# Pooling in block chains on GpSimd, two pooling steps moved, and eight weight pieces brought forward in a fused attention and MoE kernel

## The chip, the core and the metric

The kernel runs on one core of a Trainium2 chip. The metric is device time in microseconds (us) of one execution. The engines are named as the profile names them: PE (TensorE, matmul), PEld (its weight loads), DVE (VectorE), ACT (ScalarE), POOL (GpSimd) and SP (SyncE, which issues most DMAs). Each works through its own instructions in order; they wait for one another by semaphores.

## The reference

Three layers run one after the other. Attention pools keys and values by 8, the second layer sends each of 4608 tokens to one of 8 experts, the third is dense. Here is the reference with setup and argument handling cut.

```python
# attention: q, k, v are (8, 8, 576, 64), keys and values are averaged over 8 positions
k_p = k.reshape(B, H, Sp, pool, D).mean(axis=3)      # Sp = 72
v_p = v.reshape(B, H, Sp, pool, D).mean(axis=3)
scores = scale * np.matmul(q, k_p.transpose(0, 1, 3, 2))
attn = softmax(scores)
x = np.matmul(attn, v_p)                              # -> 4608 tokens x 512
# experts: each token goes to its best expert
logits = x @ w_gate
e_idx = np.argmax(logits, axis=1)
gate_w = softmax(logits)[token, e_idx]
eom = 1.0 / (1.0 + np.exp(-(x @ w_output_gate)))
for e in range(8):
    h = np.maximum(x[mask] @ w1[e], 0.0)              # 512 -> 1024
    out[mask] = gate_w * eom * (h @ w2[e])            # 1024 -> 512
# dense: w_in and w_out are float64 in memory
r = np.maximum(x @ w_in, 0.0)                         # 512 -> 2048
y = (s * (r * r) + b) @ w_out                         # 2048 -> 512
```

## The kernel before, in words

The order of the instructions on every engine is written by hand (a manual schedule); the framework only adds the semaphore waits.

**Attention** (function `attention`) loops over t = 0 to 39 in steps of one tile of 128 tokens. Four and a half tiles make a batch element b. A step of the loop transposes queries (`s1`), multiplies them with pooled keys and subtracts the row maximum (`s2`), takes the exponential, transposes it (`s3`), multiplies it with the masked values (`s4`) and divides (`s5`). Steps that prepare a batch element are put at a t by the list `sched`: `pool_k(b)` and `pool_v(b)` add the 8 positions of keys and values, in three halvings (512 to 256, to 128, to 64 columns) over five blocks of up to 128 partitions; `prep_k`, `prep_l` and `prep_v` transpose the result on PE; `mask_v` and `mask_g` write the masked values and gate columns that `s4` reads. Keys and values lie in two buffers each, `krs[b % 2]` and `vrs[b % 2]`, and a buffer's next load on the SP queue waits until it is pooled. For b = 0 and 1 the pooling is on DVE, three instructions over all blocks; for later b on POOL, where the helper `add` cuts each halving into instructions of at most 256 columns: five for the first halving, three for the second, then three (keys) or two (values). Three tiles after each group of tiles is through, a router (class `Router`) ranks the tokens by expert on DVE, a few instructions between the others; its first batch starts with lines 556 and 557.

**Experts** (function `experts`) runs 39 slots of 128 tokens with the data given (36 fixed, the rest under a condition). In a slot PE does the first product of slot i (24 matmuls of 512 columns), the second product of slot i-1 (24) and twelve transposes. POOL gathers the tokens of a later slot, loads the next expert's weights when the expert changes (line 838) and scatters the token order (`tok.order`, line 1161). Each of these DMAs is issued by POOL in its own order. Beside this, `db.step` (class `Doubles`) turns the dense layer's float64 weights into float32, piece by piece: per step one load by SP, one ACT, three DVE and two POOL instructions on 128x256 values (lines 937 to 954), and for a piece of `w_out` also a split into two parts on ACT and DVE (lines 813 and 814). `db.pieces` lists 12 pieces of `w_out` (`EARLY`), then 32 of `w_in`, then 20 of `w_out`. The first 44 are done in the expert slots: `side` calls `db.step` once in each slot and once more where i % 3 is 0. From slot 34 on `ahead` loads the dense layer's first tokens by transposing DMAs (line 1200), and after slot 35, before slot 36, it calls `dn.join` four times: two copies that put the halves of the words together (line 1210, one on ACT and one on DVE) and two multiplications (line 1213, DVE).

**Dense** (class `Dense`) runs 9 groups of 512 tokens, 16 steps f each. A step does 12 matmuls of the first product (`c1`), ReLU on ACT, square, scale and split on DVE and ACT, and 12 matmuls of the second product (`c2`) two steps later. In group 0 the steps f = 1 to `REST` each hold two more calls of `db.step`, one of them ahead of the last DVE instruction of `c1`; `REST` is half of the pieces that are left, plus one: 11. Steps 0 to 4 also reload and split the second half of `w_in` (`reload`). At f = `REST` the next group's tokens are loaded, and in the four steps after that they are joined on ACT and DVE and cut in two for PE. Later groups are joined on POOL.

Of the kernel before, what the change touches and what calls it, by code (L numbers as in the profile page):

```python
# [16 lines left out]
ALU = mybir.AluOpType  # L17
# [5 lines left out]
B, H, S, D = 8, 8, 576, 64  # L23
# [11 lines left out]
NBLK = 5  # L35
# [10 lines left out]
KB = 7 * SP // 4  # L46


def attention(ctx, tc, c, q, k, v, wg, wog, xd, lg, ro, spare, hooks):
    nc = tc.nc  # L50
# [7 lines left out]
    krs = [  # L58
        one.tile([KB, NBLK, POOL * D], F32, name="kr"),
        spare[0:KB, 0:NBLK * POOL * D].rearrange("p (j f) -> p j f", j=NBLK),  # L60
    ]
    vrs = [one.tile([P, NBLK, POOL * D], F32, name=f"vr{i}") for i in range(2)]
# [16 lines left out]
    def load_kv(b, src, dst, n, j0=0, j1=NBLK):  # L79
        rows = src[b].rearrange("h (s r) d -> (h s) (r d)", r=POOL)  # L80
        j2 = min(j1, 4)
        nc.sync.dma_start(
            out=dst[0:n, j0:j2, :], in_=rows[j0 * n:j2 * n].rearrange("(j p) f -> p j f", p=n)
        )
        if j1 == NBLK:
            nc.sync.dma_start(out=dst[0:H * SP - 4 * n, 4, :], in_=rows[4 * n:H * SP])
# [36 lines left out]
    kp = {}  # L123
    vp = {}
    vt = {}

    def add(eng, out, x, y, w):

        n = out.shape[1]
        step = n if eng is nc.vector else max(1, 256 // w)  # L130
        for j in range(0, n, step):
            o, a, b = [t[:, j:min(j + step, n)] for t in (out, x, y)]
            eng.tensor_tensor(out=o, in0=a, in1=b, op=ALU.add)

    def halve(eng, t):
        add(eng, t[:, :, 0:256], t[:, :, 0:256], t[:, :, 256:512], 256)
        add(eng, t[:, :, 0:128], t[:, :, 0:128], t[:, :, 128:256], 128)

    def pool_k(b, j0=0, j1=NBLK):
        eng = nc.vector if b <= 1 else nc.gpsimd  # L140
        t = krs[b % 2][:, j0:j1]
        if j0 == 0:
            kp[b] = p2.tile([KB, NBLK, 2, D], F32, tag="kp", name="kp")
        halve(eng, t)
        x, y = [t[:, :, i:i + 64].unsqueeze(2).to_broadcast([KB, j1 - j0, 2, D]) for i in (0, 64)]
        add(eng, kp[b][:, j0:j1], x, y, 128)

    def pool_v(b):
        eng = nc.vector if b <= 1 else nc.gpsimd
        t = vrs[b % 2]  # L150
        vp[b] = vps[b % 2]
        halve(eng, t)
        add(eng, vp[b][:, 0:NBLK], t[:, :, 0:64], t[:, :, 64:128], 64)

    def prep_k(b, parts=((0, 4, 0, 7),)):

        pr = ps.tile([P, 512], F32, tag="prep", name="prk")
        kb = kbd[b % 3]
        prv = pr[:, 0:7 * SP].rearrange("p (h s) -> p h s", s=SP)

        def part(j0, j1, h0, h1):
            for j in range(j0, j1):
                nc.tensor.transpose(
                    out=pr[:, KB * j:KB * j + KB], in_=kp[b][:, j].rearrange("p t d -> p (t d)"),
                    identity=ident[0:KB, 0:KB],
                )
            copy = nc.vector.tensor_copy if j0 else nc.scalar.copy
            nc.scalar.copy(out=kb[0:64, h0:h1, 0, :], in_=prv[0:64, h0:h1])
            copy(out=kb[64:P, h0:h1, 1, :], in_=prv[64:P, h0:h1])

        return [lambda a=a: part(*a) for a in parts]
# [211 lines left out]
    def at(i, f, *a):  # L383
        sched.setdefault(i, []).append((f, a))
# [20 lines left out]
    prep_l(0)  # L405
    load_q(4)
    load_kv(1, v, vrs[1], P)
    at(1, pool_v, 0)
    at(4, pool_v, 1)
    at(2, prep_v, 0)  # L410
    at(2, mask_v, 0, 0, NBLK)
    at(3, pool_k, 1)
    at_end = {3: [lambda: prep_k(1)[0](), lambda: prep_l(1)]}
    at(5, prep_v, 1)
    at(5, mask_v, 1, 0, 3)
# [459 lines left out]
CW = 256  # L875
AHEAD = 2
NDX = 6
EARLY = 12
LO64 = 2.0 ** -15
HI64 = 2.0 ** 17 * (1.0 - 2.0 ** -24) * 0.9375  # L880

# [1 line left out]
class Doubles:  # L883
# [5 lines left out]
    def __init__(self, tc, ctx, w_in, w_out, wi):  # L889
# [3 lines left out]
        self.wi, self.wo, self.wf = wi, [], None  # L893
        self.more(ctx, EARLY * CW // DM)
        self.src = [w.bitcast(I32) for w in (w_out, w_in)]
        out = [(0, r, c) for r in range(FF // P) for c in range(DM // CW)]
        self.pieces = out[:EARLY] + [(1, r, c) for c in range(FF // CW) for r in range(DM // P)] + out[EARLY:]
        self.x, self.t, self.stores = {}, {}, []
        self.run(0, EARLY + len(self.pieces) // 2)

# [425 lines left out]
def kernel(  # L1326
# [15 lines left out]
    nc = tc.nc  # L1342
# [6 lines left out]
    kp = {}  # L1349
# [60 lines left out]
    dn = Dense(tc, wide, half, wt.a, wt.b, db, s_b, ys, out, tok)  # L1410

    def side(i, part):
        ahead(i, part)
        if part == 0:
            if i == 0:
                close_ranks(tc, c, wide(), kp)
            db.step()
        else:
            if i == 3:
                token_scale(tc, wide(), lg, kp, tok.scale)  # L1420
            if i % 3 == 0:
                db.step()
            if i > 3:
                tok.order(kp["pos"], 1 + (i % 4 == 0))

    def ahead(i, part):

        k = 2 * (i - NT + 3) + part - 2
        if k == -1:
            tok.load(kp["pos"])  # L1430
        elif 0 <= k < 4:
            dn.load(0, k)
        elif k == 4:
            for k in range(4):
                dn.join(0, k, [nc.scalar, nc.vector])

    with ExitStack() as x:
        db.wf = x.enter_context(tc.tile_pool(name="wf", bufs=1)).tile([P, DM // P, FE], F32, name="wf")
# [39 lines left out]
```

## Time and profile before

| what | value |
|---|---|
| time, median of 3 executions | 1535.36 us (1525.38 to 1536.66) |
| the profiled execution's own time | 1536.34 us |
| its span, first to last instruction | 1534.7 us |
| PE busy | 1464.4 us (95%) |
| DVE busy | 815.2 us (53%) |
| ACT busy | 522.3 us (34%) |
| POOL busy | 497.3 us (32%) |
| mean granted TensorE clock | 0.982 |

Attention fills the span up to about 213 us, the expert slots go from 216 to 727 us, the dense layer from 734 to the end. Busy time is what the profiler records for an engine's instructions; PE's ends are modelled, so that PE can show as busy where it issues few matmuls, and the number of its instructions in a stretch tells more. An idle time in square brackets stands ahead of its instruction and names what ended it. PEclk is the share of full TensorE speed that was granted: 1.00 is 2.4 GHz, and the lower level is half of it.

### The profile page before, as it was taken

The page shows a single profiled execution, that of the slowest core. Times are in us where ns is not written, and L with a number is a line of the kernel's source. Part 1 is how long each engine was busy: PE and PEld are TensorE (multiplying, and loading weights), DVE is VectorE, ACT ScalarE, POOL GpSimd, SP SyncE. Part 2 cuts the span into 40 slices and gives each one's busy share as a digit, 9 for nine tenths or more (in the row PEclk, how much of TensorE's full clock was granted, in tenths as well). Part 3 has the DMA queues.
Part 4 walks back from the last instruction along what each step waited for, and adds up shares of the span by engine and source line. Part 5 has one row for each costly group of instructions (what it writes and reads, how often), then busy time and mean ns, then how long its engine had stood idle before and what let it go on. Part 6 is the DMA issues. An engine that isn't in the chain of part 4 may idle for free.

```text
span 1534.7 us, 21105 instructions
## 1 busy us (share of the span) xinstructions
PE 1464.4 (95%) x7264; PEld 1228.2 (80%) x7264; DVE 815.2 (53%) x1503; ACT 522.3 (34%) x984; POOL 497.3 (32%) x609
## 2 busy tenths in 40 slices
PE   5979999999799999997999999999999999999997
PEld 5879988877588888886877888888888888888886
DVE  5788884475544557333896434444444434444432
ACT  3546632353433344222543222222222222222221
POOL 3964233445554455400470304040220304040100
PEclk9999999999899999998999999999999999999998
DMA  9866352265544457372423101010010101000000
GB/s 253 286 196 201 118 199 84 70 227 179 152 124 116 136 145 239 86 70 61 144 66 86 28 14 42 21 42 21 28 35 15 35 14 42 15 28 1 28 1 28
DMA packets 127401, 141.02 MB, mean 92 GB/s; under 512 B 62174, under 2 KB 84958, under 8 KB 127262
## 3 DMA queue, kind: packets, MB, share of 16 engines
q1 hardware_dynamic: 111726, 89.28, 21.3%
q0 software_dynamic: 15536, 50.12, 10.3%
q8 instruction: 59, 0.97, 0.3%
q14 instruction: 80, 0.66, 0.2%
HBM read 98.67 MB, written 31.25 MB: 85 GB/s over the span
## 4 chain that ended last, share of the span: by engine, by line
PE 45%; DVE 4%; ACT 1%; issue 1%; DMA 1%; another core or an unknown queue 0%; SPq 0%; POOLq 0%; ACTq 0%; DVEq 0%
PE po L1273 8%; PE po L1272 8%; PE po L1271 8%; PE ph L1241 8%; PE ph L1242 8%; PE ph L1240 8%; DVE gl L1260 1%; DVE r L1245 1%; DVE r L1246 1%; DVE wo L814 1%; DMA wb<-wi 0%; DVE wb L814 0%; ACT dx L937 0%; DVE dt L949 0%; DVE dy L1213 0%
## 5 line engine op out<-in xcount | busy, mean ns | idle before, releaser
L1245 DVE TENSOR_TENSOR r<-r 128x512 f32<-128x512 f32 x144 | 108.9, 756 | 301.6 <-ACT r L1244 301.4
L1283 POOL DMA_INDIRECT out<-yo,kp_pos x36 | 37.1, 1031 | 588.5 <-ACT yo L1282 521.2
L1273 PE MATMUL po<-wo,gl 128*128 128x512 f32 x560 | 218.7, 391 | 1.8 <-DVE gl L1260 1.7
L1271 PE MATMUL po<-wo,gh 128*128 128x512 f32 x560 | 217.9, 389 | 0.0
L1272 PE MATMUL po<-wo,gh 128*128 128x512 f32 x560 | 217.9, 389 | 0.0
L1046 PE MATMUL py<-wb,hh 128*128 128x512 f32 x624 | 199.0, 401 | 14.1 <-ACT wb L813 7.8
L1244 ACT ACTIVATE r<-ph 128x512 f32<-128x512 f32 x144 | 85.7, 595 | 324.6 <-PE ph L1242 324.6
L1257 ACT ACTIVATE gh<-r 128x512 fp32r<-128x512 f32 x140 | 88.5, 632 | 216.7 <-DVE r L1246 216.7
L1046 PEld LDWEIGHTS py<-wb,hh 128*128 128x128 f32 x624 | 120.9, 194 | 43.4 <-ACT wb L813 9.1
L1260 DVE TENSOR_TENSOR gl<-r,gh 128x512 fp32r<-128x512 f32 x140 | 106.9, 764 | 90.5 <-ACT gh L1257 90.5
L1015 PE MATMUL ph<-wa,xh 128*128 128x512 f32 x312 | 126.7, 406 | 0.0
L1273 PEld LDWEIGHTS po<-wo,gl 128*128 128x128 f32 x560 | 105.1, 188 | 26.5 <-DVE gl L1260 4.8
L1016 PE MATMUL ph<-wa,xh 128*128 128x512 f32 x312 | 123.1, 395 | 1.6 <-DVE wa L814 1.6
L1017 PE MATMUL ph<-wa,xl 128*128 128x512 f32 x312 | 122.9, 394 | 0.0
L1046 PE MATMUL py<-wb,hl 128*128 128x512 f32 x312 | 122.7, 397 | 0.0
L1271 PEld LDWEIGHTS po<-wo,gh 128*128 128x128 f32 x560 | 105.2, 188 | 21.6
L1272 PEld LDWEIGHTS po<-wo,gh 128*128 128x128 f32 x560 | 105.0, 188 | 21.9
L1240 PE MATMUL ph<-xdh,wa 128*128 128x512 f32 x288 | 112.2, 389 | 1.8 <-ACT xdh L813 1.8
L1241 PE MATMUL ph<-xdl,wa 128*128 128x512 f32 x288 | 112.1, 389 | 0.3 <-DVE xdl L814 0.3
L1240 PE MATMUL ph<-xdh,wb 128*128 128x512 f32 x288 | 112.0, 389 | 0.0
L1242 PE MATMUL ph<-xdh,wa 128*128 128x512 f32 x288 | 112.0, 389 | 0.0
L1241 PE MATMUL ph<-xdl,wb 128*128 128x512 f32 x288 | 112.0, 389 | 0.0
(237 smaller groups left out, 2724.1 us busy)
## 6 DMA issues: line engine op xcount, KB each, us to landing
wr<-in_moe_w POOLq DMA_DIRECT2D x56, 512.0 KB
ys<-y SPq DMA_DIRECT2D x38, 256.0 KB
xd<-x SPq DMA_DIRECT2D x36, 256.0 KB
q<-in_q SPq DMA_DIRECT2D x16, 512.0 KB
vr<-in_v SPq DMA_DIRECT2D x8, 1024.0 KB
wr<-in_moe_w SPq DMA_DIRECT2D x16, 512.0 KB
dx<-in_moe_w_out SPq DMA_DIRECT2D x32, 256.0 KB
dx<-in_moe_w_in SPq DMA_DIRECT2D x32, 256.0 KB
```

The costliest lines, as they stand in the source:

```text
L1015: nc.tensor.matmul(ph, lhsT=xh[:, k], rhs=wh[:, k, s], start=k == 0, stop=False)
L1016: nc.tensor.matmul(ph, lhsT=xh[:, k], rhs=wl[:, k, s], start=False, stop=False)
L1017: nc.tensor.matmul(ph, lhsT=xl[:, k], rhs=wh[:, k, s], start=False, stop=k == 3)
L1046: nc.tensor.matmul(py, lhsT=a, rhs=w, start=j == 0, stop=j == len(steps) - 1)
L1240: nc.tensor.matmul(ph, lhsT=wh[:, k, s], rhs=xh[:, k], start=k == 0, stop=False)
L1241: nc.tensor.matmul(ph, lhsT=wh[:, k, s], rhs=xl[:, k], start=False, stop=False)
L1242: nc.tensor.matmul(ph, lhsT=wl[:, k, s], rhs=xh[:, k], start=False, stop=k == 3)
L1245: nc.vector.tensor_tensor(out=r, in0=r, in1=r, op=ALU.mult)
L1260: nc.vector.tensor_tensor(out=gl, in0=r, in1=gh.bitcast(F32), op=ALU.subtract)
L1271: nc.tensor.matmul(o, lhsT=gh[:, s], rhs=wh, start=f == 0, stop=False)
L1272: nc.tensor.matmul(o, lhsT=gh[:, s], rhs=wl, start=False, stop=False)
L1273: nc.tensor.matmul(o, lhsT=gl[:, s], rhs=wh, start=False, stop=f == NC - 1)
```

## The change

The helpers `add` and `halve` give way to `pooled`. On DVE it issues the same three instructions; on POOL it takes one block after the other and does all three halvings of a block in a row, so that each instruction reads what the one before it has written. Fifteen instructions do a batch element's keys or values on POOL, where eleven or ten did before. `pool_v(0)` moves from DVE (t = 1) to POOL, ahead of the loop. `pool_k(1)` stays on DVE and moves from t = 3 to t = 2. `EARLY` goes from 12 to 20: eight pieces of `w_out` move from the dense layer's first group into the expert slots, `REST` becomes 7, and `side` calls `db.step` a second time in two of three slots. The first four joins go to POOL.

```diff
-    def add(eng, out, x, y, w):
+    def pooled(eng, out, t):
         n = out.shape[1]
-        step = n if eng is nc.vector else max(1, 256 // w)
-        for j in range(0, n, step):
-            o, a, b = [t[:, j:min(j + step, n)] for t in (out, x, y)]
-            eng.tensor_tensor(out=o, in0=a, in1=b, op=ALU.add)
-
-    def halve(eng, t):
-        add(eng, t[:, :, 0:256], t[:, :, 0:256], t[:, :, 256:512], 256)
-        add(eng, t[:, :, 0:128], t[:, :, 0:128], t[:, :, 128:256], 128)
+        for j in [slice(0, n)] if eng is nc.vector else [slice(j, j + 1) for j in range(n)]:
+            o, a = out[:, j], t[:, j]
+            eng.tensor_tensor(out=a[:, :, 0:256], in0=a[:, :, 0:256], in1=a[:, :, 256:512], op=ALU.add)
+            eng.tensor_tensor(out=a[:, :, 0:128], in0=a[:, :, 0:128], in1=a[:, :, 128:256], op=ALU.add)
+            x, y = a[:, :, 0:64], a[:, :, 64:128]
+            if len(o.shape) == 4:
+                x, y = [i.unsqueeze(2).to_broadcast(list(o.shape)) for i in (x, y)]
+            eng.tensor_tensor(out=o, in0=x, in1=y, op=ALU.add)
...
-        eng = nc.vector if b <= 1 else nc.gpsimd
-        t = vrs[b % 2]
         vp[b] = vps[b % 2]
-        halve(eng, t)
-        add(eng, vp[b][:, 0:NBLK], t[:, :, 0:64], t[:, :, 64:128], 64)
+        pooled(nc.vector if b == 1 else nc.gpsimd, vp[b][:, 0:NBLK], vrs[b % 2])
...
-    at(1, pool_v, 0)
+    pool_v(0)
     at(4, pool_v, 1)
     at(2, prep_v, 0)
     at(2, mask_v, 0, 0, NBLK)
-    at(3, pool_k, 1)
+    at(2, pool_k, 1)
...
-EARLY = 12
+EARLY = 20
...
-            if i % 3 == 0:
+            if i % 3 != 2:
                 db.step()
...
-                dn.join(0, k, [nc.scalar, nc.vector])
+                dn.join(0, k, [nc.gpsimd, nc.gpsimd])
```

On POOL, the pooling of the keys of b = 2 (`kr` is the key buffer, `kp` its result) stood like this; in brackets is what an instruction waits for, and Pool there is an earlier instruction of POOL itself:

```order
L133 TENSOR_TENSOR kr<-kr 126x256 [waits DMAHW1_49,DMAHW0_49,DVE_49]
L133 TENSOR_TENSOR kr<-kr 126x256 x2
L133 TENSOR_TENSOR kr<-kr 126x256 [waits DMAHW2_49,DVE_49]
L133 TENSOR_TENSOR kr<-kr 126x256 [waits DMAHW2_49]
L133 TENSOR_TENSOR kr<-kr 126x2x128 [waits Pool_49] x2
L133 TENSOR_TENSOR kr<-kr 126x128 [waits Pool_49]
L133 TENSOR_TENSOR kp<-kr 126x256 [waits PE_49,Pool_49]
L133 TENSOR_TENSOR kp<-kr 126x256 [waits Pool_49]
L133 TENSOR_TENSOR kp<-kr 126x128 [waits Pool_49]
```

Now it stands like this, after the five chains of `pool_v(0)`:

```order
L133 TENSOR_TENSOR kr<-kr 126x256 [waits DMAHW1_49,DMAHW0_49,DVE_49]
L134 TENSOR_TENSOR kr<-kr 126x128 [waits Pool_49]
L138 TENSOR_TENSOR kp<-kr 126x128 [waits PE_49,Pool_49]
L133 TENSOR_TENSOR kr<-kr 126x256
L134 TENSOR_TENSOR kr<-kr 126x128 [waits Pool_49]
L138 TENSOR_TENSOR kp<-kr 126x128 [waits Pool_49]
L133 TENSOR_TENSOR kr<-kr 126x256
L134 TENSOR_TENSOR kr<-kr 126x128 [waits Pool_49]
L138 TENSOR_TENSOR kp<-kr 126x128 [waits Pool_49]
```

Before, a wait for POOL itself was for an instruction two or three places earlier; now it is for the one just ahead, twice in each block.

On DVE, around the loop's steps t = 1 to 3 (`vr` and `vp` are the values, `wr` the keys of b = 1, `vbd` the masked values and gates, `mx` and `es` the maximum and the difference of one tile each), the order was:

```order
L133 TENSOR_TENSOR vp_154<-vr_140 128x320
L294 TENSOR_REDUCE mx<-sc 128x8
L297 TENSOR_TENSOR es<-sc,mx 128x576
L206 TENSOR_SCALAR vbd_147<-vp_154,msk 128x64 x4
L225 TENSOR_TENSOR vbd_147<-pf,msk 128x2x16
L225 TENSOR_TENSOR vbd_147<-pf,msk 128x3x16 x3
L225 TENSOR_TENSOR vbd_147<-pf,msk 128x16
L294 TENSOR_REDUCE mx<-sc 128x8
L297 TENSOR_TENSOR es<-sc,mx 128x576
L133 TENSOR_TENSOR wr_116<-wr_116 126x5x256
L133 TENSOR_TENSOR wr_116<-wr_116 126x5x128
L133 TENSOR_TENSOR kp<-wr_116 126x640
```

and is now:

```order
L288 TENSOR_REDUCE mx<-sc 128x8
L291 TENSOR_TENSOR es<-sc,mx 128x576
L200 TENSOR_SCALAR vbd_147<-vp_154,msk 128x64 x4
L133 TENSOR_TENSOR wr_116<-wr_116 126x5x256
L134 TENSOR_TENSOR wr_116<-wr_116 126x5x128
L138 TENSOR_TENSOR kp<-wr_116 126x640
L219 TENSOR_TENSOR vbd_147<-pf,msk 128x2x16
L219 TENSOR_TENSOR vbd_147<-pf,msk 128x3x16 x3
L219 TENSOR_TENSOR vbd_147<-pf,msk 128x16
L288 TENSOR_REDUCE mx<-sc 128x8
L291 TENSOR_TENSOR es<-sc,mx 128x576
```

The list before begins with the last of the three instructions of `pool_v(0)`; all three have left DVE. Those of `pool_k(1)` (`wr` and `kp`) came after the five instructions of `mask_g` (`vbd` from `pf`) and one more pair of `mx` and `es`; now they come ahead of them.

On ACT, between slots 35 and 36 of the experts (`xh` and `y` belong to slot 35's work, `hs` is the ReLU of slot 36's first product, the branch opens slot 36), the order was:

```order
L813 ACTIVATE xh_2787<-pt 128x512
L993 COPY y<-py 128x512
L1210 COPY dy<-dy 128x512 x4
L1125 COMPARE_AND_BRANCH
L1019 ACTIVATE hs_2790<-ph 128x512
```

and is now:

```order
L859 UNCONDITIONAL_BRANCH x2
L807 ACTIVATE xh_2853<-pt 128x512
L987 COPY y<-py 128x512
L1119 COMPARE_AND_BRANCH
L1013 ACTIVATE hs_2856<-ph 128x512
```

The four copies of the joins have left ACT; DVE loses its four copies and eight multiplications at the same place, and POOL has all sixteen ahead of its branch.

## Rows read from the trace of the kernel before

**Rows 1.** Busy time by stretch; instruction counts in brackets

```profile
core 0: us, PE busy (x) PEld busy (x) DVE busy (x) ACT busy (x) POOL busy (x), PEclk, DMA share, GB/s
0.00:40.00 40.00, 23.04 (x121) 21.13 (x122) 24.03 (x52) 13.28 (x30) 15.08 (x44) 0.91 0.98 254
400.00:440.00 40.00, 33.77 (x148) 27.25 (x147) 17.03 (x27) 12.54 (x21) 15.74 (x18) 0.87 0.56 170
680.00:720.00 40.00, 34.34 (x153) 28.18 (x152) 13.39 (x25) 9.50 (x16) 1.97 (x3) 0.91 0.31 79
840.00:880.00 40.00, 40.00 (x178) 33.10 (x178) 16.72 (x23) 9.13 (x15) 15.22 (x18) 1.00 0.13 37
```

**Rows 2.** Timeline of PE, attention: start, us, what, idle before and releaser

```profile
22.86 0.55 PE L193 MATMUL prv<-ident,vp 128*128 128x128 f32 x3 [2.56 <-DVE vp L133]
33.04 0.65 PE L163 MATMUL prk<-ident,kp 126*128 126x126 f32 x4 [2.32 <-DVE kp L133]
86.53 3.63 PE L344 MATMUL pv<-vbd,eT 128*128 128x162 f32 x12 [8.77 <-DVE vbd L225]
92.53 1.96 PE L344 MATMUL pv<-vbd,eT 128*128 128x162 f32 x12
123.11 0.49 PE L193 MATMUL prv<-ident,vp 128*128 128x128 f32 x3
```

**Rows 3.** Timeline of DVE, attention

```profile
19.94 2.34 DVE L133 TENSOR_TENSOR vr<-vr 128x1280 f32<-128x1280 f32 x2
29.78 2.34 DVE L133 TENSOR_TENSOR wr<-wr 126x1280 f32<-126x1280 f32 x2
32.16 0.83 DVE L133 TENSOR_TENSOR kp<-wr 126x640 f32<-126x640 f32 x1
75.32 9.54 DVE L557 TENSOR_TENSOR rcand<-lg,rmx 128x64 f32<-128x64 f32 x1
121.58 0.26 DVE L557 TENSOR_TENSOR rcand<-lg,rmx 128x64 f32<-128x64 f32 x1
```

**Rows 4.** Timeline of POOL, attention

```profile
33.25 5.23 POOL L133 TENSOR_TENSOR kr<-kr 126x256 f32<-126x256 f32 x8 [23.39 <-DMA kr<-in_k]
84.36 0.42 POOL L187 COPY kbm<-kbd 64x288 f32<-64x288 f32 x1
```

**Rows 5.** POOL groups by line and shape, first 560 us

```profile
L133 POOL TENSOR_TENSOR vr<-vr 128x256 f32<-128x256 f32 x42 | 29.0, 729 | 0.2
L133 POOL TENSOR_TENSOR vr<-vr 128x128 f32<-128x128 f32 x6 | 2.8, 460 | 0.0
L133 POOL TENSOR_TENSOR vp<-vr 128x64 f32<-128x64 f32 x6 | 1.9, 324 | 0.0
```

**Rows 6.** Timeline of POOL, one later join of the dense stage

```profile
846.24 1.45 POOL L1210 COPY dy<-dy 128x512 uint16<-128x512 uint16 x2
847.77 1.88 POOL L1213 TENSOR_TENSOR dy<-dy,ds 128x256 f32<-128x256 f32 x2
849.60 1.64 POOL L1210 COPY dy<-dy 128x512 uint16<-128x512 uint16 x2
```

**Rows 7.** Timelines of PE and ACT around the first joins

```profile
694.59 1.12 PE L1029 MATMUL th<-ident,hs 128*128 128x128 f32 x4 [4.81 <-ACTq L865]
696.56 1.12 PE L1029 MATMUL th<-ident,hs 128*128 128x128 f32 x4 [0.86 <-DVEq L865]
...
690.82 0.76 ACT L1210 COPY dy<-dy 128x512 uint16<-128x512 uint16 x1 [5.13 <-DMA dy<-ys]
693.95 0.58 ACT L1019 ACTIVATE hs<-ph 128x512 f32<-128x512 f32 x1
```

**Rows 8.** Busy time in the last part of the first dense group

```profile
785.00:826.00 41.00, 38.78 (x167) 30.52 (x166) 34.72 (x70) 18.34 (x38) 14.94 (x15) 1.00 0.37 80
```

**Rows 9.** Timelines of POOL and DVE, expert stage

```profile
405.43 0.99 POOL L1161 DMA_INDIRECT tab<-tok,kp_pos  x1 [4.97 <-DMA tab<-tok,kp_pos]
...
410.54 0.84 DVE L945 TENSOR_SCALAR dt<-dt 128x256 int32<-128x256 int32 x1 [5.10 <-POOL dt L939]
```

More of the change, by code (lines that the diff above doesn't have):

```diff
@@ L125, in attention @@
     vt = {}
-    def add(eng, out, x, y, w):
+    def pooled(eng, out, t):
         n = out.shape[1]
-        step = n if eng is nc.vector else max(1, 256 // w)
-        for j in range(0, n, step):
-            o, a, b = [t[:, j:min(j + step, n)] for t in (out, x, y)]
-            eng.tensor_tensor(out=o, in0=a, in1=b, op=ALU.add)
-    def halve(eng, t):
-        add(eng, t[:, :, 0:256], t[:, :, 0:256], t[:, :, 256:512], 256)
-        add(eng, t[:, :, 0:128], t[:, :, 0:128], t[:, :, 128:256], 128)
+        for j in [slice(0, n)] if eng is nc.vector else [slice(j, j + 1) for j in range(n)]:
[6 more added lines that the diff above has]
+            eng.tensor_tensor(out=o, in0=x, in1=y, op=ALU.add)
     def pool_k(b, j0=0, j1=NBLK):
-        eng = nc.vector if b <= 1 else nc.gpsimd
-        t = krs[b % 2][:, j0:j1]
         if j0 == 0:
             kp[b] = p2.tile([KB, NBLK, 2, D], F32, tag="kp", name="kp")
-        halve(eng, t)
-        x, y = [t[:, :, i:i + 64].unsqueeze(2).to_broadcast([KB, j1 - j0, 2, D]) for i in (0, 64)]
-        add(eng, kp[b][:, j0:j1], x, y, 128)
+        pooled(nc.vector if b <= 1 else nc.gpsimd, kp[b][:, j0:j1], krs[b % 2][:, j0:j1])
     def pool_v(b):
-        eng = nc.vector if b <= 1 else nc.gpsimd
-        t = vrs[b % 2]
         vp[b] = vps[b % 2]
-        halve(eng, t)
-        add(eng, vp[b][:, 0:NBLK], t[:, :, 0:64], t[:, :, 64:128], 64)
+        pooled(nc.vector if b == 1 else nc.gpsimd, vp[b][:, 0:NBLK], vrs[b % 2])
     def prep_k(b, parts=((0, 4, 0, 7),)):
```

## The prediction

> **What bounds the kernel now.** I first read the page's busy shares: PE 95%, no other engine above 53%. So the question is where PE is held up, and I went through the windows of 40 us, then the timelines of PE around each hole. In the dense layer a full stretch looks like 840 to 880 us: 178 matmuls in 40 us, 0.225 us each, clock 1.00 [rows 1]. Three kinds of stretch fall short. At the front PE is busy for 23.0 of 40 us; at 400 to 440 it issues few matmuls at a clock of 0.87; at 680 to 720 it is busy 34.3 us at 0.91 [rows 1]. The timeline of PE gives the holes of attention: 2.56 us for the pooled values of b = 0, 2.32 us for the pooled keys of b = 1, and 8.77 us for a gate column from DVE [rows 2]. After the last one the twelve matmuls of `s4` take 3.63 us, where the same twelve take 1.96 us a step later [rows 2]: the lower clock level for a while.
>
> The timeline of DVE explains them. The first two holes are DVE's own pooling: 2.34 us and a last halving for the values, 2.34 + 0.83 = 3.2 us for the keys [rows 3]. The third hole is one small comparison of the router, line 557 with 128x64 values: 9.54 us, where its next run takes 0.26 [rows 3]. It begins at 75.32 and ends at 84.86; POOL changes from two-input additions to a one-input copy at 84.36, and that copy ends at 84.78 [rows 4]. So I read the 9.5 us as DVE waiting for POOL's train of additions.
>
> **Part 1, chains.** By the means of one block on POOL, 0.73, 0.46 and 0.32 us [rows 5], and a wait for the instruction just ahead, a block of values takes longer than its three instructions. What such a wait costs shows in a later join: two copies from 846.24 take 1.45 us, and the multiplication that needs both starts at 847.77, 0.08 us after their end [rows 6]. A block is then 0.73 + 0.08 + 0.46 + 0.08 + 0.32, about 1.65 us, and b's values 8.2 us; keys end with 128 columns instead of 64 and take about 9. Before, the first two halvings were 5.2 us [rows 4] and the last one to two more. Each pooling on POOL grows by almost 2 us, and POOL is idle for at least 0.08 us after two of every three instructions.
>
> In those gaps a waiting DVE instruction can go ahead. Then the 8.77 us of PE go, and the slow matmuls behind it, 3.63 - 1.96 = 1.67 us: 10.4 us. The cost is that POOL gets late. Its chains can't start before 33.25, when the keys of b = 2 land [rows 4]. From there to the values of b = 5 there are eight poolings, 4 x 17.2 = 68.8 us, and eight copies of 0.42 [rows 4], with their waits some 4 us: 106 us. PE wants them at 123.11 now [rows 2]; with 10.4 us of this part and 4.5 of the next gone, at 108. The cover is 2 us, so each wait of DVE's additions against POOL shows soon. I charge 1.5 us. **-9.0**; bounds: 0 if the stall stays, -10.4 if POOL is never late.
>
> Here a rule of the Trainium skill speaks against the reading. "SBUF - State Buffer", section "Who interferes with whom", says that a DVE instruction with two SBUF inputs and a GpSimd instruction that reads SBUF share a port, and that the one that issues first holds it for its whole instruction. By this DVE would wait for one addition, at most 0.73 us, and not 9.54 across a dozen; then something else held line 557 and this part would bring nothing. The row differs from the rule in length, not in kind, and the end of the stall at the end of the train makes me go by the row; the rest is rival A.
>
> **Part 2, first values on POOL, second keys sooner.** About 1.7 MB of keys and queries and 1.2 MB of values come first; at 254 GB/s [rows 1] they are in at about 12 us (estimate). POOL is free from 33.25 - 23.39 = 9.9 us [rows 4], so the chain ends near 20.5 instead of 22.8, and the first hole shrinks by some 2.3 us. DVE then has `pool_k(1)`, 3.2 us, ahead of `mask_g` for `s4(0)`; PE loses about 0.9 us there. The second hole, 2.32, goes, since the keys are pooled by about 26. That makes -3.7, and the front's clock of 0.91 [rows 1] will give some of it back, say 0.8. **-4.5**; bounds: if the values landed as late as DVE takes them now (19.94 [rows 3]), the chain would end at 28 and the first hole grow by 5, so +1 in all; at best -7.
>
> **Part 3, first joins on POOL.** ACT's copy at 690.82 had waited 5.13 us for a transposing load; behind it in ACT's order stood slot 36's ReLU, which ran at 693.95, and PE's transposes of it waited 4.81 us, and 0.86 us more for the half that DVE makes [rows 7]. That is 5.67 us, and the clock of 0.91 over 40 us [rows 1] means about 7 us at half speed, 3 us of work or a little more: 8.5 us. On POOL the same join takes 849.60 - 846.24 = 3.4 us [rows 6], four of them 13.4 us. If the loads land no later than now, POOL is done by about 707. The cut of the joined tiles comes after slot 38, two slots later, so I count about ten us of cover. Behind the joins on POOL stands the gather of a slot that isn't used before the end. PE has no other wait for POOL there. **-8.5**; bounds 0 and -9.
>
> **Part 4, eight pieces less in the dense layer's first group.** DVE sets the pace there: 785 to 826 has 167 matmuls in 41 us [rows 8], where a full stretch would have 182 [rows 1], 15 short, 3.4 us. With `REST` = 7 the double steps of `db` end before this stretch, the joins of group 1 come four steps sooner, and PE's own matmuls bound it. What the first steps lose with `reload` stays. **-3.5**; bounds -1 and -6.
>
> **Part 5, the same pieces in the expert slots.** In slots of the usual kind PE hides them: DVE works about 17 of 40 us even at 400 to 440 [rows 1]. But in that stretch experts change almost each slot and POOL is late already: a scatter waited 4.97 us for an older one, and DVE's step at 410.54 waited 5.10 us for POOL's half of an earlier step [rows 9]. Two or three more steps fall here, each with two POOL instructions in front of scatters and weight loads. I take **+3**, between nothing (the weights' transfers bound these slots anyway) and +10 (each extra step holds a weight load for one such wait of 5 us, twice).
>
> The sum is -9.0 - 4.5 - 8.5 - 3.5 + 3 = -22.5 us. From the profiled execution's 1536.3 us this gives **1514 us**. That execution stands 1 us above the median of the three; one of the three was 10 us faster, and I can't tell which of the holes it lacked.
>
> **The rivals.**
> A. The stall of the comparison stays, because POOL's train was not its cause or because DVE loses the port all the same. For it: other DVE instructions get through POOL's trains quickly. Against it: the end at 84.36 to 84.86. Part 1 is then +1.5 instead of -9: about 1524 us. The skill's rule above leads here.
> B. The expert slots lose as much as their bound, +10 instead of +3, and a little more from slots with a lone change of expert: about 1522 us. For it: POOL late at 405 us. Against it: most of those waits are for transfers, which don't grow.
> C. A wait for the instruction just ahead costs POOL far more than 0.08 us, and POOL becomes what attention waits for. There are 80 of them up to the values of b = 5. With e us more for each, POOL is 80e late, less 2 us of cover; from e = 0.3 on this eats the 22 us gain. If a wait cost as much as the second halving, 0.46 [rows 5], e is 0.38 and PE stands for 28 us: about 1542 us, slower than before. Against it: the 0.08 of rows 6.
> D. The joins' loads land so late on POOL's side that the cut after slot 38 waits in the place of slot 36, and part 3 gives nothing: about 1522 us. Against it: the cover of two slots.
>
> **How the numbers follow.** Forecast 0.64 (its own range 1504 to 1520), A 0.13, B 0.11, C 0.05, D 0.07. The range of 1502 to 1527 takes in A, B and D as well as both bounds of parts 2, 4 and 5, and leaves out C and combinations of two rivals. A measurement of this kernel can tell about 1%, 15 us. The forecast lies 1.4% below 1535.4, and only its slow edge comes within 1%; A, B and D lie within 1% of the median. Faster by over 1%: 0.64. Within 1%: 0.30. Slower: 0.06, which is C and a little for several things at once.
>
> **What would show it.** Part 1: line 557's first run takes under 2 us, PE has no hole over 3 us between 60 and 100 us, and the POOL instructions of a chain start about 0.08 us after one another's end. Where POOL is late, PE's transposes of pooled keys or values name POOL as what ended their idle time. Part 2: PE's first hole under 1 us, the second gone. Part 3: no idle time at the transposes of slot 36, and POOL's joins done well before the cut. Part 4: PE at full count from about the tenth step of the dense layer on. Part 5: the sum of PE's idle time between 320 and 450 us, where more than 10 us over now would make rival B true. The forecast is wrong if attention is not at least 9 us shorter, or if the step from slot 36 to slot 37 still takes over 14 us.

## The result and the profile after

The changed kernel takes 1515.6 us, the median of 7 runs (1513.15 to 1519.97); the kernel before, run beside it, 1533.87 (7 runs, 1525.38 to 1537.30). The ratio is 0.9901 with a 95% interval of 0.9871 to 0.9930: 1% faster, 18.3 us by the medians. The profiled execution took 1513.15 us with a span of 1511.5, against 1536.34 and 1534.7. The forecast was 1514. The total is right; two of its five terms are off by about 4 us and two more by 2 to 3, and most of what follows is about these. The forecast took its 22.5 us off the profiled execution's 1536.3, while the median of the kernel before was 1533.87 here, so that 2.4 us of the agreement lie in the starting point.

Where the 23.2 us between the two profiled spans lie, by the first matmul of each stage in the timeline of PE (us from the span's start, the differences worked out):

| | before | after | difference |
|---|---|---|---|
| attention, to slot 0's first expert matmul | 216.40 | 206.94 | -9.46 |
| slots 0 and 1 | 21.11 | 20.26 | -0.85 |
| slots 2 to 35 | 441.10 | 440.68 | -0.42 |
| slots 36 and 37 | 33.06 | 24.49 | -8.57 |
| from slot 38 to the first dense matmul | 22.85 | 23.75 | +0.90 |
| dense, to the end | 800.22 | 795.36 | -4.86 |

The four stretches of [rows 1] in the changed kernel, and the one of [rows 8] at the same distance from the first dense matmul (busy time by stretch; the counts in brackets are instructions):

```profile
core 0: us, PE busy (x) PEld busy (x) DVE busy (x) ACT busy (x) POOL busy (x), PEclk, DMA share, GB/s
0.00:40.00 40.00, 23.69 (x141) 21.33 (x141) 24.92 (x55) 15.22 (x35) 21.62 (x56) 0.96 0.97 252
400.00:440.00 40.00, 34.39 (x157) 28.17 (x158) 21.20 (x36) 13.82 (x24) 23.59 (x24) 0.91 0.52 180
680.00:720.00 40.00, 37.09 (x166) 30.55 (x165) 17.18 (x23) 14.32 (x23) 8.63 (x11) 0.91 0.23 72
...
766.60:807.60 41.00, 41.00 (x183) 33.95 (x182) 22.29 (x40) 14.01 (x24) 0.00 (x0) 1.00 0.22 52
```

The front issues 141 matmuls where it issued 121. The dense stretch has 183 where it had 167, and PE shows no idle time in it.

The router's comparison (line 557 before, 551 now) took 9.54 us [rows 3]. In the timelines of DVE and POOL after, it and the router's next two-input instruction read:

```profile
73.55 0.26 DVE L551 TENSOR_TENSOR rcand<-lg,rmx 128x64 f32<-128x64 f32 x1
...
73.93 0.53 DVE L555 TENSOR_TENSOR rcand<-rcand,desc 128x64 f32<-128x64 f32 x1
...
73.66 0.72 POOL L133 TENSOR_TENSOR kr<-kr 126x256 f32<-126x256 f32 x1
74.46 0.46 POOL L134 TENSOR_TENSOR kr<-kr 126x128 f32<-126x128 f32 x1
```

The comparison takes its 0.26 us. Line 555, 0.21 us where nothing is in its way, takes 0.53 and ends at 74.46, at the end of POOL's idle time between 74.38 and 74.46. So a wait for POOL is still there, and it lasts to the next gap of the chain. The chain is as forecast: an instruction starts 0.08 us after the one it waits for has ended.

PE in attention, after. These answer [rows 2]:

```profile
21.02 0.33 PE L187 MATMUL prv<-ident,vp 128*128 128x128 f32 x1 [0.31 <-POOL vp L138]
...
26.07 2.05 PE L338 MATMUL pv<-vbd,eT 128*128 128x162 f32 x12 [1.39 <-DVE vbd L219]
...
61.60 2.02 PE L338 MATMUL pv<-vbd,eT 128*128 128x162 f32 x12 [1.60 <-DVE x L366]
...
98.55 0.46 PE L276 MATMUL sc<-kbm,qT 128*64 128x144 f32 x2 [1.01 <-POOL kbm L182]
99.51 1.19 PE L276 MATMUL sc<-kbm,qT 128*64 128x144 f32 x14 [0.50 <-POOL kbm L182]
```

The holes of 2.56, 2.32 and 8.77 us are gone. In the first's place stands 0.31 us, `mask_g` costs 1.39, and there are three new ones, at 60, 97 and 99 us. The second and third name a product of POOL that the prediction had counted only as time: the copies `kbm` of `prep_m`. The hole at 60 us leads to SP. DVE's line 366 waits for a store of `x` to leave its tile, and SP had spent 6.48 us on that store (timelines of DVE, SP and POOL):

```profile
60.76 0.69 DVE L366 TENSOR_TENSOR x<-pv,rec 128x512 f32<-128x512 f32 x1 [1.89 <-DMA xd<-x]
...
46.48 6.48 SPq L369 DMA_DIRECT2D xd<-x  x1
53.06 0.38 SPq L82 DMA_DIRECT2D vr<-in_v  x1
...
51.40 0.32 POOL L138 TENSOR_TENSOR vp<-vr 128x64 f32<-128x64 f32 x1
```

The load behind the store wants blocks that POOL is done with at 51.72, before the store's own time ends at 52.97. So it is not shown that POOL's lateness held the store; what did stays open. The expectation of `later` below reads this row as a wait for POOL.

The first joins, now on POOL, and PE's transposes of slot 36, which answer [rows 7]:

```profile
685.09 1.43 POOL L1207 TENSOR_TENSOR dy<-dy,ds 128x256 f32<-128x256 f32 x2
...
678.89 1.03 PE L1023 MATMUL th<-ident,hs 128*128 128x128 f32 x8
```

All eight transposes run in one go. POOL is done with the four joins at 686.5, two slots ahead of the cut.

### The profile page after: what moved, and what is told of

It is laid out like the page before. It is cut to its first block, busy times and chain, and to the rows that moved or that the text cites. A ratio compares the mean times of both kernels' runs of the same rounds, so it can differ in the third digit from the quotient of the medians.

```text
span 1511.5 us, 21197 instructions
## 1 busy us (share of the span) xinstructions
PE 1455.3 (96%) x7264; PEld 1224.2 (81%) x7264; DVE 794.6 (53%) x1488; ACT 520.4 (34%) x980; POOL 525.9 (35%) x694
## 4 chain that ended last, share of the span: by engine, by line
PE 50%; DVE 1%; ACT 0%; issue 0%; DMA 0%; POOLq 0%; ACTq 0%
PE po L1267 8%; PE ph L1236 8%; PE ph L1234 8%; PE ph L1235 8%; PE po L1265 8%; PE po L1266 8%; PE py L1040 1%; DVE r L1239 0%; DVE wb L808 0%; DVE gl L1254 0%; DVE wo L808 0%; DVE r L1240 0%; DMA out<-yo,kp_pos 0%; ACT dx L931 0%; ACT wo L807 0%
```

## Experiments

Each kernel below is the changed kernel with the edit shown, but for `chains`, which starts from the kernel before. Not all of them ran on the same chip, so the ratio to the runs of the kernel before on the same chip stands with each time.

| kernel | median us | runs | ratio to before, 95% interval | slot 0 begins | slots 2 to 35 | slots 36, 37 | dense |
|---|---|---|---|---|---|---|---|
| changed | 1515.60 | 7 | 0.9901 (0.9871 to 0.9930) | 206.94 | 440.68 | 24.49 | 795.36 |
| `train` | 1520.75 | 10 | 0.9949 (0.9920 to 0.9978) | 212.93 | 442.80 | 24.49 | 796.08 |
| `pairs` | 1523.72 | 10 | 0.9954 (0.9925 to 0.9983) | 218.00 | 441.11 | 24.49 | 795.40 |
| `breaks` | 1534.54 | 10 | 1.0022 (0.9995 to 1.0049) | 226.86 | 440.99 | 24.49 | 795.40 |
| `later` | 1513.54 | 7 | 0.9898 (0.9864 to 0.9932) | 201.72 | 441.37 | 24.49 | 795.40 |
| `joins` | 1523.43 | 10 | 0.9947 (0.9921 to 0.9974) | 208.49 | 438.71 | 32.60 | 795.82 |
| `firsts` | 1518.24 | 10 | 0.9899 (0.9874 to 0.9924) | 207.18 | 444.94 | 24.49 | 796.25 |
| `pieces` | 1513.92 | 4 | 0.9878 (0.9822 to 0.9935) | 208.39 | 434.96 | 24.49 | 800.91 |
| `chains` | 1521.05 | 10 | 0.9921 (0.9891 to 0.9952) | 206.80 | 435.42 | 32.78 | 800.32 |
| `again` | 1516.61 | 6 | 0.9908 (0.9872 to 0.9944) | 208.81 | 442.82 | 24.49 | 795.96 |
| `copies` | 1513.08 | 6 | 0.9895 (0.9857 to 0.9933) | 204.20 | 440.70 | 24.49 | 795.40 |
| `later_again` | 1514.59 | 6 | 0.9900 (0.9864 to 0.9936) | 202.48 | 441.68 | 24.49 | 795.63 |
| `spread` | 1517.12 | 8 | 0.9922 (0.9891 to 0.9952) | 203.79 | 447.70 | 24.49 | 796.43 |

The last four columns are from the one profiled execution of each, in us; "dense" is from its first matmul to the end. The expectations below count the slots one lower from the second on: their "slots 1 to 35" are the column of 2 to 35, their "35 to 37" that of 36 and 37.

### What holds the comparison: `train`, `pairs`, `breaks`

`train` has the old order by stages on POOL, one block to an instruction:

```diff
-        for j in [slice(0, n)] if eng is nc.vector else [slice(j, j + 1) for j in range(n)]:
-            (three halvings of block j)
+        for g in [[slice(0, n)]] if eng is nc.vector else [[slice(j, j + 1) for j in range(n)]]:
+            for s in range(3):
+                for j in g:
+                    (halving s of block j)
```

> The changed kernel, but POOL pools stage by stage over all five blocks again (five additions of 256 columns, five of 128, five last ones), so that an instruction never waits for the one just ahead of it; the rest of the change stays. Theory (an unbroken train of two-input additions on POOL holds a DVE instruction with two SBUF inputs until the train ends): of the router's first instructions on DVE, about 73 to 85 us, one takes over 5 us again, PE has a hole of more than 5 us there with a slow stretch behind it, and the time is 1515.6 + 7 to 10 = about 1523 to 1526 us. Rival A (the train was not the cause): none of them takes over 1 us, POOL is 1 to 2 us earlier at each pooling, and the time is 1512 to 1516.

The hold is back, on another instruction. In the timelines of DVE, POOL and PE of `train`:

```profile
82.21 7.21 DVE L627 CAST rri<-rrank 128x8 int32<-128x8 f32 x1
...
88.98 0.41 POOL L181 COPY kbm<-kbd 64x288 f32<-64x288 f32 x1
89.45 0.43 POOL L182 COPY kbm<-kbd 64x288 f32<-64x288 f32 x1
...
91.60 3.57 PE L338 MATMUL pv<-vbd,eT 128*128 128x162 f32 x12 [6.94 <-DVE vbd L219]
```

A cast of 8 columns, 0.16 us at other times, takes 7.21 and ends at 89.42. POOL's 14 additions and the copy behind them follow one another without idle time; the first is the 0.06 us between 89.39 and 89.45, where the second copy waits for the first. The hold ends in it. In the kernel before, the 9.54 us ended in such a gap too: POOL's first copy ends at 84.78 [rows 4], DVE's comparison at 84.86, and between them POOL's next copy starts:

```profile
84.84 0.42 POOL L188 COPY kbm<-kbd 64x288 f32<-64x288 f32 x1
```

In `train` PE has its hole of 6.94 us and then the twelve matmuls at the lower clock level, 3.57 us as in [rows 2]. Rival A falls. The price is 6.0 us of attention in the profile (4.1 against `again`) and 5.2 us by the medians, or 7.4 by the ratios; of the 7 to 10 expected that is the low end or less. Without links POOL is earlier, and PE has no hole at 97 us in `train`: undoing the chains also gives back what they cost.

`pairs` keeps nearly the order of the chains, but no instruction waits for the one just ahead:

```diff
+        for g in ... [[slice(j, j + 1) for j in g] for g in ((0, 1), (2, 3, 4))]:
+            for s in range(3):
+                for j in g:
+                    (halving s of block j)
```

> The changed kernel, but POOL's blocks are pooled in two interleaved groups (blocks 0 and 1, then 2, 3 and 4: each stage of a group before its next stage). An addition then waits for the one two or three ahead, which has ended, and POOL has no idle 0.08 us; the order is still nearly block by block. Theory that the idle gaps let DVE in: the gaps of 0.08 us are gone from POOL's rows, the hold is back at more than 4 us in one of DVE's instructions of the router, and the time is 1520 to 1526. Rival (the new order of the blocks, or the shift in time, did it, and not the gaps): no DVE instruction of the router over 1 us, each pooling about 1 us shorter than in chains, 1512 to 1516.

```profile
76.05 5.58 DVE L551 TENSOR_TENSOR rcand<-lg,rmx 128x64 f32<-128x64 f32 x1
...
78.16 3.31 POOL L138 TENSOR_TENSOR vr<-vr 128x256 f32<-128x256 f32 x6
```

The comparison is held for 5.58 us, another instruction of the router (line 562) for 3.72, and at 129.53 a step that splits expert weights (line 844) takes 2.52 instead of 0.68. POOL's six additions from 78.16 on take 3.31 us with no idle time between them. So it is not the order of the blocks or their place in time that helps: it is the 0.08 us in which POOL is idle. The two long holds end at 81.64 and 87.64, where POOL has no gap. PE also had a hole of 4.38 us at 58 us here, of the kind at 60 us above.

`breaks` takes the order of `train` and puts a copy of one column, which waits for no addition, behind each:

```diff
+                    if eng is nc.gpsimd:
+                        eng.tensor_copy(out=brk[:, 1:2], in_=brk[:, 0:1])
```

> The changed kernel with the stage by stage order of the run 'train', and behind each of POOL's additions a copy of one column (one input, 128x1), which does not wait for the addition. Theory 1 (a waiting DVE instruction gets in as soon as POOL runs something other than a two-input addition): no DVE instruction of the router over 1 us; a pooling costs 7 us plus 15 small copies of some 0.1 us, as long as in chains, and the time is 1513 to 1517. Theory 2 (only an idle POOL lets it in): one DVE instruction over 5 us, 1521 to 1527.

```profile
118.35 8.48 DVE L555 TENSOR_TENSOR rcand<-lg,rmx 128x64 f32<-128x64 f32 x1
...
125.86 0.73 POOL L138 TENSOR_TENSOR vr<-vr 128x256 f32<-128x256 f32 x1
126.52 0.19 POOL L140 COPY brk<-brk 128x1 f32<-128x1 f32 x1
126.66 0.49 POOL L138 TENSOR_TENSOR vr<-vr 128x128 f32<-128x128 f32 x1
```

Theory 2 holds: changing to a one-input instruction lets nothing in. DVE was held three times, the longest past 13 of the small copies: for 8.48 us, and two others took 3.97 and 3.23 us. The long hold ends at 126.83 with no idle time on POOL. It got in beside an addition that took 0.49 us instead of 0.45. So without a gap DVE does get in at some point, here and in `pairs` after 3 to 8.5 us; what decides when stays open. Each copy puts the next addition off by 0.12 us, almost 2 us to a pooling, and the kernel is as slow as the one before.

### Part 1 alone: `chains`

The kernel before with the new `pooled` and nothing else (values of b = 0 on DVE).

> The kernel before with the chains alone: part 1. Theory of the prediction: no hold of a DVE instruction over 1 us in attention, POOL late by little, slot 0's first expert matmul at 216.4 - 9 = 207.4 us, time 1533.9 - 9 = 1525. Rival (the chains make POOL late, and the waits for SP's queue and for POOL's copies give back more than 1.5 us): slot 0 at 209 to 213 us, 1527 to 1531.

Slot 0 begins at 206.80, 9.6 us earlier than in the kernel before, for which 9.0 was forecast. The time fell by more, 13.6 us by the medians (1534.63 in 25 runs of the kernel before beside it, 1521.05) and 12.1 by the ratio. In the profile slots 2 to 35 are 5.7 us shorter as well, with the same pieces in the same places; the prediction had no term for that. Over all kernels of this document the holds go with the order on POOL: in none of the ten profiles with chains is an instruction of DVE in attention more than 0.7 us longer than the median of its line and shape, and in each of the four without them one is held for over 5 us.

The chains' lateness shows here too, without part 2. PE waits for the copies `kbm` at 97 us exactly as in the changed kernel:

```profile
98.27 0.46 PE L276 MATMUL sc<-kbm,qT 128*64 128x144 f32 x2 [1.01 <-POOL kbm L182]
```

### Part 2 undone: `firsts`

```diff
-    pool_v(0)
+    at(1, pool_v, 0)
-    at(2, pool_k, 1)
+    at(3, pool_k, 1)
```
and `pool_v` takes DVE for b = 0 again.

> The changed kernel with the first values pooled on DVE at step 1 and the keys of b = 1 at step 3 again: part 2 undone alone. Theory of the prediction (part 2 is worth 4.5 us to the end): slot 0's first expert matmul comes 4 to 5 us later than 206.9, 1520 us. Rival (POOL sets the pace from its first keys on, which land at 33.3 us with part 2 or without it, so most of the gain at the front is only waited away later): the matmuls of the first steps are 4 us later, those from about 75 us on only 1 to 2 us, slot 0 at 208 to 209, 1516.5 to 1518 us.

Undoing part 2 moves nothing at slot 0 (207.18, and 206.80 in `chains`, which does not have it either; 206.94 to 208.81 in the four kernels that have it and no other change in attention), and the ratio is the same, 0.9899 to 0.9901. The first transposes of the query tiles 8, 13, 18 and 19, from the timelines of PE (us):

| | tile 8 | tile 13 | tile 18 | tile 19 | slot 0 |
|---|---|---|---|---|---|
| `firsts` (no part 2) | 52.87 | 75.55 | 98.38 | 103.45 | 207.18 |
| `chains` (no part 2) | 51.14 | 73.81 | 96.62 | 102.94 | 206.80 |
| changed | 49.71 | 74.31 | 96.90 | 103.22 | 206.94 |
| `joins` | 49.14 | 72.66 | 96.06 | 105.00 | 208.49 |
| `pieces` | 49.30 | 72.76 | 95.57 | 104.75 | 208.39 |
| `again` | 46.66 | 73.24 | 96.14 | 105.29 | 208.81 |
| `copies` | 47.60 | 71.97 | 95.48 | 99.76 | 204.20 |
| `later` | 48.74 | 72.12 | 93.85 | 98.39 | 201.72 |

At tile 8 the four kernels with part 2 are 1.4 to 6.2 us ahead of the two without. At tiles 13 and 18 their mean lead is down to about 1.4 us, and the two groups overlap; where the rest went differs from kernel to kernel. One step later `joins`, `pieces` and `again` are 1.3 to 2.4 us behind, and the changed kernel is level. Between the two stands PE's wait for the copies `kbm`. The first of these starts on POOL at 97.3 to 98.1 us in all six, with part 2 or without, so whoever arrives earlier waits longer.

### Where it goes: `again`, `copies`, `later`, `later_again`

`copies` moves `prep_m` one step ahead for b from 2 on; `later` adds the loads:

```diff
-        at(TPG * (b // 2) + (5 if b > 1 else 3 + b), prep_m, b)
+        at(TPG * (b // 2) + (4 if b > 1 else 3 + b), prep_m, b)
-        ... (f - 13, f - 8, f - 12, f - 7))
+        ... (f - 11, f - 8, f - 10, f - 7))
```

> The changed kernel with two changes of its schedule in attention: from b = 2 on the loads of raw keys and values are issued two steps later (on SP they now wait up to 6.5 us for POOL to free the tile, and stores of x stand behind them; one of these stores held DVE's line 366 for 1.89 us and PE for 1.60 at 59.99 us), and the two pairs of copies of prep_m one step earlier, in front of POOL's pooling of the keys of b = 5 (PE waited 1.01 and 0.50 us for them from 97.5 us). Theory (these two waits are what POOL's lateness costs): both holes gone, slot 0's first expert matmul about 3 us earlier than its 206.9 us, 1511 to 1514. Rival (POOL is late anyway and its next product is waited for instead): another hole of 1 us or more before 110 us, 1514.5 to 1517.

> The changed kernel itself, beside the three that follow, since the runs of an earlier call may have been on another chip: 1513 to 1518 us. Theory (POOL's lateness meets PE at the copies of line 182): its profile has a hole of 1 to 2.3 us of PE before a matmul of these copies at about 97 us again. A hole at 60 us behind a late store of x may be there or not.

> The changed kernel with one edit of the run 'later' alone: prep_m's copies one step earlier from b = 2 on, in front of POOL's pooling of the keys of b = 5. Theory (these copies are the place where attention gives back what part 2 gained: at 93 us the kernels with part 2 are 2.6 to 3.1 us ahead of the one without it, at 103 us 1 to 1.5 us behind): the hole at 97 us is gone, slot 0's first expert matmul 2.5 to 5 us earlier than in 'again', and the time 2 to 5 us below it. Rival (POOL's next product is late as well): slot 0 less than 1.5 us earlier.

> The kernel of the run 'later' again, beside the changed kernel on the same chip. Theory (the loads' place on SP's queue costs something of its own): 0.5 to 2 us below 'copies', and no PE hole at 60 us. Rival: equal to 'copies' within 1 us.

In `again` the two copies stand behind the last block of the keys of b = 5, and PE waits 2.23 us for the first pair (timelines of POOL and PE); in `copies` the same sixteen matmuls run in one go:

```profile
97.65 0.45 POOL L138 TENSOR_TENSOR kp<-wr 126x128 f32<-126x128 f32 x1
98.05 0.42 POOL L181 COPY kbm<-kbd 64x288 f32<-64x288 f32 x1
98.52 0.42 POOL L182 COPY kbm<-kbd 64x288 f32<-64x288 f32 x1
...
99.00 0.46 PE L276 MATMUL sc<-kbm,qT 128*64 128x144 f32 x2 [2.23 <-POOL kbm L182]
...
96.04 1.20 PE L276 MATMUL sc<-kbm,qT 128*64 128x144 f32 x16
```

From tile 18 to tile 19 it is 9.15 us in `again` and 4.28 in `copies`: 4.9 us for holes of 2.73, the rest being slow matmuls behind them (granted clock 0.74 from 102 to 106 us in the windows of `again`). In the changed kernel and in `chains` the step takes 6.32 us, with holes of 1.51 and the clock at 1.00 behind them. Slot 0 begins 4.6 us earlier in `copies` than in `again`, 2.7 earlier than in the changed kernel's own profile; by the theory that was 2.5 to 5. `copies` was not run without part 2, and `chains` pays the same wait, so how much of this is part 2's own gain is not shown. The three profiles with the later loads (`later`, `later_again` and `spread`) begin slot 0 another 0.4 to 2.5 us earlier and have no hole at 60 us; but of the kernels without that edit only the changed one and `pairs` have one. By time `copies` and `later_again` lie 3.5 and 2.0 us below `again`, with 6 runs each that spread over 6 to 10 us. The profiles show the gain; the times can't tell these kernels apart, nor prove any faster than the changed kernel.

### Part 3 undone: `joins`

```diff
-                dn.join(0, k, [nc.gpsimd, nc.gpsimd])
+                dn.join(0, k, [nc.scalar, nc.vector])
```

> The changed kernel with the first dense joins back on ACT and DVE: part 3 undone alone. Theory (part 3 took away the wait of slot 36's ReLU behind a copy that waits for a transposing load): from the first expert matmul of slot 35 to that of slot 37 it is 33 us again and not 24.5, PE's transposes of slot 36 wait about 5 us, and the time is 1515.6 + 8.5 = about 1524. Rival (the loads land sooner now, since other stages moved): that stretch stays below 28 us and the time below 1519.

Slots 36 and 37 take 32.60 us instead of 24.49, and the old pair of waits is back (PE, then ACT):

```profile
684.48 1.11 PE L1023 MATMUL th<-ident,hs 128*128 128x128 f32 x4 [4.79 <-ACTq L859]
...
680.55 0.76 ACT L1204 COPY dy<-dy 128x512 uint16<-128x512 uint16 x1 [4.39 <-DMA dy<-ys]
```

The time rises by 7.8 us by the medians, 7.1 by the ratios. In the profile these two slots are 8.1 us longer.

### Parts 4 and 5: `pieces`, `spread`

```diff
-EARLY = 20
+EARLY = 12
-            if i % 3 != 2:
+            if i % 3 == 0:
```

> The changed kernel with 12 early pieces and one step of them in three slots again: parts 4 and 5 undone together. Theory (the dense layer gains, the expert slots lose nothing): from the first dense matmul to the end it is 800 us again and not 795.4, the slots 1 to 35 stay within 1 us of 440.7 us, and the time is 1520.4. Prediction's sizes (dense 3.5 us, slots 3 us): dense 799, slots 437.7, 1516. Rival B would have the slots at 431 and the time at 1510.

The dense layer takes 800.91 us again, 5.5 us more. But slots 2 to 35 take 434.96 and not 440.7, and the time is 1513.92, in 4 runs: the two parts together bring nothing that the times show. The comparison of the profiles of before and after hid this, since the kernel before had 441.10 us there with 12 pieces; `chains` and `pieces`, with the same pieces as it, have 435.42 and 434.96. All eleven kernels with 20 pieces have 438.7 to 447.7. So the price of 5.7 us rests on two profiles against these, while the kernel before lies among them.

The mechanism is like that of [rows 9], with a gather in the scatter's place. In the changed kernel one case reads (POOL, DVE, PE):

```profile
354.56 1.07 POOL L933 TENSOR_SCALAR dt<-dt 128x256 f32<-128x256 f32 x1 [5.55 <-DMA xg<-xd,kp_idx]
...
355.66 0.82 DVE L939 TENSOR_SCALAR dt<-dt 128x256 int32<-128x256 int32 x1 [6.89 <-POOL dt L933]
...
357.32 1.28 PE L1023 MATMUL th<-ident,hs 128*128 128x128 f32 x8 [3.37 <-ACT hs L1013]
```

POOL's clamp for a piece stands behind a DMA that POOL has to wait for; DVE's next instruction waits for the clamp, ACT's split of a piece for POOL's addition behind it, and behind these stand the slot's own ReLU halves, on which PE's transposes wait. From 225 to 680 us DVE's waits for that clamp are, in `pieces`, then in the changed kernel (total us, times, longest):

```profile
DVE dt L939 <- POOL dt L933: 27.9, 9, 9.3
...
DVE dt L939 <- POOL dt L933: 45.2, 12, 7.6
```

In `chains` they are 28.8 us in 9, in the kernel before 33.8 in 10, in `spread`, the kernel with the longest slots, 35.2 in 11. So their sum does not measure the price; it counts only where PE is reached. `spread` was to bring the dense layer's gain without this price, on the schedule of `later`:

```diff
-            if i % 3 != 2:
+            if not 8 <= i <= 15 and i % 4 != 3:
```

> The kernel of the run 'later' with the same 20 early pieces, but the additional steps of the double-precision pieces kept out of slots 8 to 15 (two steps in a slot for 21 of the other 28 slots). Theory (part 5 costs 5.5 us, and it costs it where the experts change in each slot: slots 1 to 35 took 440.7 us with 20 pieces and 435.0 with 12): slots 1 to 35 in 433 to 436 us, the dense layer still 795.4, and the time 4 to 6 us below 'later_again'. Rival (the slots' length goes with the number of pieces, or with when the slots begin, and not with the place of the steps): 439 us or more, time within 2 us of 'later_again'.

It failed by its second half. An undisturbed slot takes 12.25 us. In slots 10 to 15, where steps were taken out, what goes beyond that fell from 23 us in `later_again` to 16. But slots 23, 24 and 29 to 31 now lose 15 us where only slot 23 lost 2, and slots 2 to 35 take 447.7 us. At slot 30 (POOL, DVE, PE of `spread`):

```profile
602.29 1.00 POOL L1155 DMA_INDIRECT tab<-tok,kp_pos  x1 [6.80 <-DMA tab<-tok,kp_pos]
604.24 1.07 POOL L933 TENSOR_SCALAR dt<-dt 128x256 f32<-128x256 f32 x1 [0.95 <-DMA xg<-xd,kp_idx]
...
605.34 0.82 DVE L939 TENSOR_SCALAR dt<-dt 128x256 int32<-128x256 int32 x1 [6.91 <-POOL dt L933]
...
607.28 1.12 PE L1023 MATMUL th<-ident,hs 128*128 128x128 f32 x4 [5.78 <-DVE hs L1015]
```

A second scatter waits 6.80 us for the first, and the clamp stands behind it. The time is 2.5 us above `later_again` by the medians, not 4 to 6 below. So a step of a piece costs where its clamp comes behind a scatter that has to wait, and this can be in any slot. Why `pieces` and `chains` have fewer of these waits than the kernel before was not tried.

## Why the prediction was right, and where its terms were not

| part | forecast | by the runs | from |
|---|---|---|---|
| 1 chains | -9.0 | -9.6 in attention, -12 to -13.6 in all | `chains` |
| 2 first values, second keys | -4.5 | about 0 | `firsts` |
| 3 joins | -8.5 | -7.1 to -7.8 | `joins` |
| 4 dense layer | -3.5 | -5.5 | `pieces` |
| 5 expert slots | +3 | +5.7 in the profile | `pieces` |

The terms of the last column come to some -19 to -21 us, the two medians of the result to -18.3; they need not add up, since parts 1 and 2 meet at the same POOL.

**Part 1.** The mechanism was right: `train` and `pairs` bring the hold back, and its end at POOL's first gap, in `train` and in the kernel before, says why the chains help. Rival C had no ground, since a link costs 0.08 us. Line 557's run under 2 us and no hole over 3 us between 60 and 100 us came out as said. Not foreseen was that the expert slots gain too. With `chains` they are 5.7 us shorter, and DVE's waits for the clamp fall from 33.8 to 28.8 us; why is open, since one profile of each kernel is all there is.

Here the rule of the Trainium skill, "SBUF - State Buffer", section "Who interferes with whom", can be put beside rows. It says that the two engines share a port pair, that casts and scalar operations of DVE can need it in their faster modes as two-input instructions do, and that the first to issue keeps it for the whole of its instruction. The kinds agree: a comparison and a cast were held. The length does not: DVE was held for 7.21 us across 14 additions and a copy of POOL, each 0.41 to 0.72 us. In these runs a waiting DVE instruction was passed over by POOL's next one again and again, for up to 9.54 us, where that followed without a gap. In the other direction the rule fits. In the changed kernel POOL's addition at 36.19 took 1.58 us instead of 0.46 beside one DVE addition that ran from 35.73 to 37.46.

**Part 2.** This is the step that failed. "The cover is 2 us" set POOL's lateness against the values of b = 5, which PE wants at 108 us. PE wants a product of POOL earlier than that: the copies of `prep_m` at 97 us, which POOL's order has behind the pooled keys of b = 5. The eight copies were in the sum as 0.42 us of POOL's time each, not as something to be waited for. POOL begins its keys of b = 2 at 33.64 us, as before, since these still wait for their load [rows 4], so an earlier PE only meets it sooner. The 1.5 us charged for lateness are near what this wait costs with the chains alone, 2.0 us from tile 18 to 19 in `chains`; with part 2 they became 2.0 in the changed kernel and 4.6 to 4.9 in `joins`, `pieces` and `again`. About half of the lead at the front is gone by tile 13 already, and no run here puts it down to one place. Nor is it shown that lateness reached PE through SP's queue as well. Part 2's two signs, on the first two holes, came out as said, and still the term was lost.

**Part 3.** Right in place and size, 8.1 us in the two slots. The windows show the clock of 0.91 unchanged from 680 to 720, because that stretch now holds the lower level behind the wait at the end of the slots, from 704.86 on (2.91 us), which came after 720 before (3.19 us); from 680 to 704 it is 1.00.

**Parts 4 and 5.** Both were larger than forecast, inside their bounds, and of opposite sign: -0.5 forecast, about zero measured. Rival B's mechanism is seen in the rows; by the profile of `pieces` its price is a little over half of the 10 us. The sign named for it, idle time of PE from 320 to 450 us, could not have told: the kernel before happened to have nearly as much (holes over 0.8 us: 8.7 us in all, against 11.9 after).

So 1514 was met in part by luck: some 4.5 us too much in part 2 stood against 3 to 5 too little in part 1, and the starting point was 2.4 us above the median.

## What to carry to other kernels

When an engine is slowed on purpose, list each of its products with the time at which someone waits for it, and set its new lateness against the earliest; the product that the loop is named after need not be that one. A part's gain is known only when that part alone is undone: here two terms were wrong by about 4 us each and cancelled, and a comparison of before and after showed nothing of a price in the expert slots. Where two engines share a resource, look at whether the one that runs leaves gaps, not at how long its instructions are.

## What was not expected of the hardware

A DVE instruction of 0.16 us, a cast of 8 columns, was held for 7.21 us by back-to-back work on POOL, and a comparison of 0.26 us for 8.48 us, across one-input copies. A gap of 0.06 us on POOL was enough to let the waiting one in. The kernel before spread over 20 us in the 25 runs beside `chains` (1519.85 to 1539.60), `chains` over 8 in 10 (1516.54 to 1524.18). That holds of different length are the cause of this spread is not shown, since each kernel has one profile.
